# Four tags of accumulators shared out anew, row numbers read at once, and token columns written later, in one fused attention, experts and MLP kernel

## The chip, the cores and the metric

The kernel runs on one core of one Trainium2 chip. The metric is the device time of one execution in microseconds (us), the median of several executions. The engines are named as in the profile: PE is TensorE's matmul and PEld its weight load, DVE is VectorE, ACT is ScalarE, POOL is GpSimd, and SP is SyncE, which here only issues transfers.

## The reference

Three layers follow one another. The output of the first is flattened to 2304 tokens of 512 values.

```
# 1. attention, 4 x 8 heads, 576 positions of 64, causal window of 128, linear bias
scores = where(mask, q @ k.T / 8 + bias, -1e9);  x = softmax(scores) @ v
# 2. eight experts, each token goes to one of them
logits = x @ w_gate                      # 512 x 8
expert_idx = argmax(logits, axis=1);     gate_w = softmax(logits)[expert_idx]
for e in range(8):
    xe = x[expert_idx == e]
    out[expert_idx == e] = gate_w * (maximum(xe @ w1[e], 0) @ w2[e])   # 512 x 1024, 1024 x 512
# 3. one MLP for all tokens
r = maximum(out @ w_in, 0);  result = (r * r) @ w_out                  # 512 x 2048, 2048 x 512
```

## The kernel before, in words

**Three stages.** Attention takes the first 160 us or so, the experts run from there to about 377 us, and the MLP from there to the end. The experts' stage is where the change lies. Products are made of f16 halves: a value is split into a high half and a low half, and a product is three matmuls (high by high, high by low, low by high).

**Rows of an expert.** While attention runs, scatters (line 478) write each token's number into a list in DRAM, one stretch of the list for each expert. They run a second time for the last tokens ("late"), to write the gate's weight beside the number. The expert stage takes a fixed number of rows of each expert's list (384, 384, 352, 352, 304, 256, 256, 224), in pieces of 128 or fewer. `prep(e)` reads the row numbers of expert e from that list (line 989, a transfer that POOL issues). `gather(e)` turns them into indices (line 995) and fetches the tokens' rows by indirect transfers, one for each piece (line 787, POOL). `columns(e)` copies an expert's stretch of the list to the place where the last stage looks up to which token a column belongs (line 730, POOL).

**One expert.** `turn` turns a gathered piece over by eight PE transposes (line 795) into a buffer that ACT copies out (line 796). `s1` makes the first product in eight blocks, fc from 0 to 7 (lines 804 to 806). ACT writes the high half with the relu (line 807), DVE the low half (line 808). `s2` makes the second product with four accumulators side by side: in each of eight blocks, three matmuls into each of them (lines 858 to 860). At its end ACT copies the four to `yT` (line 863).

**PSUM.** Four tags a, b, c and d have two buffers each. `s1` takes a and b in turn, and the transposed pieces take d. A tag's buffers go round: whoever asks for a tag gets the older buffer, and waits until its last reader is done.

**Weights.** Each expert has eight pieces of weights. SP loads a piece (line 756), ACT writes its high half (line 778), DVE its low half (line 779). The next expert's pieces are loaded and split while the present expert computes. Between them lie the steps of `wide()`, which load and decode the weights of the third stage (line 875 loads; lines 880 to 882 and 903 to 906 are on DVE, 911 and 927 on ACT). Each engine takes its instructions strictly in its own order, which a scheduler wrote before the run: an instruction that waits holds up all behind it on that engine.

**The seam to the third stage.** During experts 6 and 7 `norm` finds scales for the outputs (line 1141 multiplies them in, on DVE) and `wide1` starts the MLP's first products (line 1187). They take PSUM through `bank`, which goes round a, b and c, or a and b alone where `self.narrow` is set.

Of the kernel before, what the change touches and what calls it, by code (L numbers as in the profile page):

```python
# [22 lines left out]
N, DM, E, F, F2 = 2304, 512, 8, 1024, 2048  # L23
P = 128
# [69 lines left out]
class K:  # L94
# [754 lines left out]
    def s2(self, ws, hts, at, n, then=None):  # L849

        nc = self.nc
        ys = [self.psum(t, [P, n]) for t in "ccab"]
        for fc in range(8):
            hh, hl = hts[fc][:, 0, :n], hts[fc][:, 1, :n]
            for d, py in enumerate(ys):
                o = fc % 2 * DM + d * P
                wh, wl = (ws[fc // 2][:, a, o:o + P] for a in range(2))
                nc.tensor.matmul(py, wh, hh, start=fc == 0, stop=False)  # L858
                nc.tensor.matmul(py, wl, hh, start=False, stop=False)  # L859
                self.last_mm = nc.tensor.matmul(py, wh, hl, start=False, stop=fc == 7)  # L860
            if fc == 7:
                for d, py in enumerate(ys):
                    nc.scalar.copy(self.yT[:, d, bass.ds(at, n)], py)  # L863
            if then is not None and fc % 2 == 1:
                then(fc // 2)
# [70 lines left out]
    def wide(self, k=1):  # L936
        def store():
            while len(self.stored) > (2 if self.steps and self.steps[0][0] != self.in_step else 0):
                self.stored.pop(0)()

        for _ in range(k):
            store()
            if self.finish:
                self.finish()
                self.finish = None
            if self.steps:
                f, *a = self.steps.pop(0)
                self.finish = f(*a)
# [23 lines left out]
    def experts(self, stack):  # L972
        nc, tc, cp = self.nc, self.tc, self.cp
        mp = self.mp = stack.enter_context(tc.tile_pool(name="mp", bufs=2))
        self.dec = mp.tile([P, 1024], U32, name="dec", bufs=1)
        self.work = mp.tile([P, 7680], F32, name="work", bufs=1)
        self.open_wide(stack)
        ids, idt, idx = self.list, self.idt, self.idx
        w = self.w_first
        wide = self.wide  # L980
        xgs = {}

        def blocks(e):
            return [(c, min(P, ROWS[e] - c * P)) for c in range(EB if e == 0 else 0, -(-ROWS[e] // P))]

        def prep(e):

            c0, c1 = blocks(e)[0][0], blocks(e)[-1][0] + 1
            dma = nc.gpsimd.dma_start(idt[:, e, c0:c1], ids[:, bass.ds(self.ev[e], 1), c0:c1].rearrange("p e a o -> p (e a) o"))
            for sc in self.scatters if e == 0 else ():  # L990
                self.behind(dma, sc)

        def gather(e):
            c0, c1 = blocks(e)[0][0], blocks(e)[-1][0] + 1
            nc.gpsimd.tensor_scalar(idx[:, e, c0:c1], idt[:, e, c0:c1, 0], float(N - 1), None, op0=ALU.min)
            xgs[e] = [self.gather_x(idx[:m, e, c:c + 1]) for c, m in blocks(e)]

        def turn(xt, e, c):
            if c < len(xgs[e]):
                g = xgs[e][c]  # L1000
                self.transpose_x(g, xt[:, :, c * P:c * P + g.shape[0]], nc.scalar.copy)

        prep(0)
        prep(1)
        gather(0)
        gather(1)
        self.places()
        with tc.issue_after(self.last_gather.ins):
            for f in self.late:
                f()  # L1010
        wide(2)
        self.s2([w[2, 0, k] for k in range(4)], self.hte, 0, EB * P, lambda d: wide())
        xt = self.new_xf(P)
        self.transpose_whole(xgs[0][0], xt)
        self.offsets()
        for e in range(E):
            W = ROWS[e] - blocks(e)[0][0] * P
            more = e + 1 < E
            if more:
                nxt = self.xt(e + 1)  # L1020
            if e == 2:
                self.overflow_table()
            if e == 7:
                for _ in self.wo_tiles(KEPT, lambda: self.ring(F16, [P, 2048])):
                    pass
            hts = []
            for fc in range(8):
                ht = self.hts(e, W)[fc]
                if e == 0:
                    self.s1_whole(fc, w[1, e, fc // 2], xt, ht, W)  # L1030
                else:
                    self.s1(fc, w[1, e, fc // 2], xt[:, :, :W], ht, W)
                hts.append(ht)
                if fc % 2 == 1 and more and e > 0:
                    w[1, e + 1, fc // 2] = self.load_w(1, e + 1, fc // 2)
                if fc in STEPS[e][0]:
                    wide()
                if fc in (3, 5, 7) and more:
                    turn(nxt, e + 1, fc // 2 - 1)
                if e == 7 and fc == 2:  # L1040
                    next(nrm)

            def then(d):
                if more:
                    w[2, e + 1, d] = self.load_w(2, e + 1, d)
                if e + 2 < E:
                    if d == 0:
                        prep(e + 2)
                    if d == 2:
                        gather(e + 2)  # L1050
                if d in STEPS[e][1]:
                    wide()
                if e == 6 and d != 2:
                    next(nrm)
                if e == 7 and d == 0:
                    with tc.issue_after(self.last_mm.ins):
                        tc.mark_branch_hint_location("overflow", "LikelyTaken", [mybir.EngineType.PE])
                if d == 3 and e < 7:
                    self.columns(e)
                    if e == 6:  # L1060
                        self.columns(7)

            self.narrow = e == 6
            if e == 6:
                nrm = self.norm(0, 24576, 14336)
            if e == 7:
                self.wide1(0, 0)
            self.s2([w[2, e, k] for k in range(4)], hts, self.off[e], W, then)
            xt = nxt

# [309 lines left out]
    def moe2(self):  # L1380
        NG, tc = NT // GT, self.tc
        self.overflow()
        nrm = {1: self.norm(1, 7168, None)}
        next(nrm[1])

        def first(k):
            self.wide()
            next(nrm[1])

        self.load_columns()  # L1390
        self.wide1(0, 1, first)
        self.turn_columns()
        while self.finish:
            self.wide()
        self.fetch_out()
        def at(*key):
            for n in MIXES.get(key, ()):
                if n in mixing:
                    for _ in mixing.pop(n):
                        pass  # L1400
                else:
                    mixing[n] = self.mix(n)
                    next(mixing[n])

        mixing = {}
        for G in range(NG):
            more, far = G + 1 < NG, G + 2 < NG
            nr = nrm[G + 2] = self.norm(G + 2, None, None) if far else iter([None] * 9)

            def step():  # L1410
                with tc.issue_after(self.end_act.ins), tc.issue_after(self.end_dve.ins):
                    next(nr)

            if G < SG:
                self.wide2(G, 0, lambda k: step() if k != 1 else None)
            else:
                self.seven(G, 0, lambda k: step() if k == 5 else None)
            at(G, 0)
            if more:
                self.wide1(G + 1, 0, lambda k: step() if k == 0 or G >= SG and k == 1 else at(G, 1) if k == 1 else None)  # L1420
            if G < SG:
                self.wide2(G, 1)
                if G + 1 == SG:
                    self.narrow = True
            else:
                self.seven(G, 1, lambda k: step() if k in (0, 1) else None)
            at(G, 2)
            if more:
                self.wide1(G + 1, 1, lambda k: step() if G >= SG and k == 0 else None)
            at(G, 3)  # L1430
# [60 lines left out]
```

## Time and profile before

| | |
|---|---|
| time, median of 3 runs | 748.61 us (748.33 to 751.21) |
| time of the profiled execution | 751.45 us |
| its span, first to last instruction | 749.6 us |
| mean granted TensorE clock | 0.984 of full speed |
| PE busy | 712.6 us, 95% |
| DVE busy | 576.8 us, 77% |
| ACT busy | 468.8 us, 63% |
| POOL busy | 206.5 us, 28% |

The span is what the trace holds; 1.85 us of the execution lie outside it. A row of a timeline says when an instruction started, how long it took, its engine, its line, what it wrote and read, and in brackets how long the engine had been idle before it and what ended the wait. A busy share over the whole span is a mean over three stages with different limits, so the rows below are from the stretch from 169 us to 377 us.

### The profile page before, as it was taken

What the parts mean: (1) busy time and instruction counts of PE and PEld (TensorE: products, weight loads), DVE (VectorE), ACT (ScalarE), POOL (GpSimd) and SP (SyncE); (2) the same over time, 40 slices, a digit from 0 to 9 for tenths busy, and PEclk for the clock granted to TensorE, in tenths of its full rate; (3) what the DMA queues carried; (4) which work ended last, traced back from release to release, by engine and by line L of the source; (5) the groups of instructions that cost most, each with busy time, mean ns of one, the idle gap of its engine ahead of it and who ended that gap; (6) DMA issues with size and microseconds to landing.
All of it is one profiled execution on the core that took longest, in us unless ns stands there. A gap on an engine that the chain in (4) does not pass through costs nothing. (4 is left out here: it accounts for less than half of the span.)

```text
span 749.6 us, 19619 instructions
## 1 busy us (share of the span) xinstructions
PE 712.6 (95%) x7979; PEld 603.5 (81%) x7979; DVE 576.8 (77%) x1442; ACT 468.8 (63%) x772; POOL 206.5 (28%) x247
## 2 busy tenths in 40 slices
PE   6899999999888999999999999999999999999996
PEld 5799899888655666788898566677899999999995
DVE  5788888864778999969986966758678787878672
ACT  5688888943457655657555664656657575757561
POOL 4573522345252401000000245523411111111011
PEclk9899999989999999999999999999999999999998
DMA  8798203876899887367704000000000000000000
GB/s 299 289 365 234 81 29 68 278 163 172 239 305 299 283 263 240 125 220 241 241 5 141 31 26 6 2 30 1 30 2 30 2 30 2 30 2 30 2 30 29
DMA packets 37416, 91.71 MB, mean 122 GB/s; under 512 B 5305, under 2 KB 16075, under 8 KB 37307
## 3 DMA queue, kind: packets, MB, share of 16 engines
q1 hardware_dynamic: 31563, 75.77, 32.1%
q0 software_dynamic: 5760, 14.65, 6.0%
q8 instruction: 64, 1.05, 0.6%
q14 instruction: 29, 0.24, 0.1%
HBM read 77.54 MB, written 13.04 MB: 121 GB/s over the span
## 5 line engine op out<-in xcount | busy, mean ns | idle before, releaser
L1187 PEld LDWEIGHTS <-wi 128*128 128x128 f16 x3024 | 170.6, 98 | 3.6 <-issue 2.3
L1323 PEld LDWEIGHTS <-wr 128*128 128x128 f16 x1008 | 98.1, 98 | 12.1 <-issue 0.7
L1187 PE MATMUL ps_a<-work,wi 128*128 128x128 f16 x1344 | 84.2, 219 | 0.0
L1187 PE MATMUL ps_b<-work,wi 128*128 128x128 f16 x1272 | 79.7, 219 | 0.4 <-ACTq L1075 0.4
L1211 DVE TENSOR_TENSOR wr<-work,wr 128x1024 f16<-128x1024 f32 (+1 forms) x72 | 70.4, 1001 | 11.0 <-ACT wr L1210 10.8
L1215 ACT ACTIVATE work<-work 128x1024 f32<-128x1024 f32 x36 | 38.1, 1057 | 54.8 <-DVE work L1207 54.8
L315 PE MATMUL ps_a<-yT,wr 128*128 128x192 f32 (+2 forms) x288 | 66.6, 352 | 5.4 <-DMA wr<-in_q_dram 5.2
L1210 ACT CAST wr<-work 128x1024 f16<-128x1024 f32 (+1 forms) x72 | 59.9, 832 | 17.1 <-DVE work L1230 7.6
L327 ACT ACTIVATE pb<-pb,nm 128x192 f32<-128x192 f32 (+2 forms) x144 | 56.5, 433 | 11.6 <-DVE nm L320 10.8
L320 DVE CUSTOM_DVE_ANT_0 pb<-ps_a,bias 128x192 f32<-128x192 f32 (+2 forms) x144 | 44.4, 327 | 16.1 <-PE ps_a L315 10.2
L778 ACT ACTIVATE wr<-rw 128x1024 f16<-128x1024 f32 x40 | 42.2, 1058 | 22.1 <-DMA rw<-in_w_dram 21.5
L1351 POOL DMA_INDIRECT out_dram<-o,oid x18 | 25.8, 1436 | 102.0 <-ACT o L1349 67.4
L779 DVE SCALAR_TENSOR_TENSOR wr<-rw,wr 128x1024 f16<-128x1024 f32 x40 | 48.8, 1221 | 5.0 <-ACT wr L778 5.0
L315 PEld LDWEIGHTS ps_a<-yT,wr 128*128 128x128 f32 x288 | 47.1, 206 | 6.4 <-DMA yT<-in_k_dram 5.5
L1286 POOL TENSOR_TENSOR yT<-wr 128x512 f32<-128x512 f16 x8 | 10.4, 1294 | 148.9 <-ACTq L1075 116.0
L338 PE MATMUL ps_b<-cst,pb 128*128 128x128 f32 x256 | 45.1, 288 | 0.5 <-ACT pts L342 0.4
L804 PE MATMUL ps_a<-work,wr 128*128 128x352 f16 (+4 forms) x112 | 34.1, 304 | 7.0 <-ACT yT L863 5.6
L1216 ACT ACTIVATE work<-work 128x1024 f32<-128x1024 f32 x36 | 38.0, 1057 | 1.1
L787 POOL DMA_INDIRECT xg<-xd,idx x21 | 26.8, 1274 | 35.6 <-PE ps_d L795 26.5
L1235 DVE TENSOR_TENSOR work<-work 128x512 f32<-128x512 f32 x18 | 13.3, 739 | 29.8 <-ACT work L1204 29.8
L859 PEld LDWEIGHTS <-wr 128*128 128x128 f16 x288 | 28.2, 98 | 9.8 <-issue 2.6
L858 PE MATMUL ps_c<-work,wr 128*128 128x352 f16 (+5 forms) x128 | 35.9, 283 | 0.0
(307 smaller groups left out, 2005.8 us busy)
## 6 DMA issues: line engine op xcount, KB each, us to landing
rw<-in_w_dram SPq DMA_DIRECT2D x40, 512.0 KB, 5.4
wi<-in_w_dram SPq DMA_DIRECT2D x20, 512.0 KB, 5.0
rw<-in_wo_dram SPq DMA_DIRECT2D x16, 512.0 KB, 4.7
rw<-in_wi_dram SPq DMA_DIRECT2D x32, 256.0 KB, 5.2
wr<-in_q_dram SPq DMA_DIRECT2D x14, 512.0 KB, 12.8
xd<-xhl POOLq DMA_DIRECT2D x16, 256.0 KB, 7.8
rw<-in_v_dram SPq DMA_DIRECT2D x12, 325.0 KB, 6.4
yT<-in_k_dram SPq DMA_DIRECT2D x4, 576.0 KB, 8.7
```

The source lines that it names most:

```text
L315: nc.tensor.matmul(ps[:, s, first:hi], q[g, u, hh // 4][:, hh % 4, s if u < 4 else 0, :], self.kt[g, hh // 2][:, hh % 2, key0:key0 + hi - ...
L320: self.last_ttr = nc.vector.tensor_tensor_reduce(out=pb[:, s, first:hi], in0=ps[:, s, first:hi], in1=self.bias[:, hh, first - lo:192], sca ...
L327: self.last_exp = nc.scalar.activation(pb[:, s, first:hi], pb[:, s, first:hi], AF.Exp, bias=nm[:, s:s + 1], scale=-1.0)
L338: nc.tensor.transpose(pt[:, t, :, s, :], pb[:, s, t * P:(t + 1) * P], self.idf)
L778: self.nc.scalar.activation(t[:, 0], st, AF.Copy, scale=sc)
L779: self.nc.vector.scalar_tensor_tensor(t[:, 1], st, sc, t[:, 0], op0=ALU.mult, op1=ALU.subtract)
L1187: self.nc.tensor.matmul(ps[:, j], w[:, kp, a, w0 * P:(w0 + 1) * P], v[:, 2 * x + kp], start=kp + b == 0, stop=kp == 1 and b == 2)
L1210: self.end_act = self.fin_act = nc.scalar.copy(hi, src)
L1211: self.end_dve = self.fin_dve = V.tensor_tensor(lo, src, hi, op=ALU.subtract)
L1215: nc.scalar.activation(ci, ci, AF.Relu)
L1216: nc.scalar.activation(ci, ci, AF.Square, scale=0.5)
L1323: nc.tensor.matmul(ps[n], x[:, v, j], y[j][:, w], start=m + i + j == 0, stop=m == 1 and i == 2 and j == 3)
```

## The change

The second product's accumulators are taken from tags c and d (two each) and no longer from c, a and b. The transposes of the next expert's pieces, also in d, come after blocks 2, 4 and 6 instead of 3, 5 and 7 (for expert 0 they stay). The row numbers of all eight experts are read one after another before the first gather, and no longer two experts ahead. The token columns are written at the end of experts 5 and 6. `bank` takes only a and b during both experts 6 and 7.

```diff
     def s2(self, ws, hts, at, n, then=None):
...
-        ys = [self.psum(t, [P, n]) for t in "ccab"]
+        ys = [self.psum(t, [P, n]) for t in "ccdd"]
...
         prep(0)
-        prep(1)
+        for e in range(1, E):
+            prep(e)
         gather(0)
         gather(1)
...
-                if fc in (3, 5, 7) and more:
-                    turn(nxt, e + 1, fc // 2 - 1)
+                if more and fc in ((3, 5, 7) if e == 0 else (2, 4, 6)):
+                    turn(nxt, e + 1, (fc + 1) // 2 - (2 if e == 0 else 1))
...
                 if e + 2 < E:
-                    if d == 0:
-                        prep(e + 2)
                     if d == 2:
                         gather(e + 2)
...
-                if d == 3 and e < 7:
-                    self.columns(e)
-                    if e == 6:
-                        self.columns(7)
-
-            self.narrow = e == 6
+                if d == 3:
+                    for f in {5: range(6), 6: (6, 7)}.get(e, ()):
+                        self.columns(f)
+
+            self.narrow = e >= 6
...
         self.overflow()
         nrm = {1: self.norm(1, 7168, None)}
+        self.narrow = False
```

Where an instruction stands is decided by the scheduler, so the diff alone does not show it. Lines above 1041 keep their numbers; those from 1126 to 1375 are two lower in the changed kernel, so that line 1141 becomes 1139.

The first place is POOL's order as the experts' stage begins: the reads of row numbers (L989), the conversion to indices (L995), the gathers (L787, into buffers `xg`). Before, the last of the two reads and what follows it:

```order
L989 ISA
L989 DMA ids_385<-ids_77 128x3x2
L995 TENSOR_SCALAR idx_386<-ids_385 128x1
L787 DMA xg_3356<-xd_76,idx_386 128x1024
L995 TENSOR_SCALAR idx_386<-ids_385 128x3
L787 DMA xg_3359<-xd_76,idx_386 128x1024
L787 DMA xg_3361<-xd_76,idx_386 128x1024
```

And now, the last of the eight reads and what follows it:

```order
L989 ISA
L989 DMA ids_385<-ids_77 128x2x2
L995 TENSOR_SCALAR idx_386<-ids_385 128x1
L995 TENSOR_SCALAR idx_386<-ids_385 128x3 x3
L787 DMA xg_3362<-xd_76,idx_386 128x1024
L787 DMA xg_3365<-xd_76,idx_386 128x1024
L787 DMA xg_3367<-xd_76,idx_386 128x1024
L787 DMA xg_3369<-xd_76,idx_386 128x1024
```

Six reads were put ahead of the first gather, and so were the conversions for experts 1, 2 and 3, which wait for the reads to land. The copies of the columns still stand soon after the first gathers in POOL's order.

The second place is ACT's order in the first product of expert 1: splits of weights (L778, from `rw` or a borrowed `wi` buffer), the relu (L807), the copies of the transposed pieces (L796, 96 columns for the last piece of expert 2). Before:

```order
L778 ACTIVATE wr<-rw 128x1024 x2
L807 ACTIVATE work<-ps_a 128x384
L778 ACTIVATE wr<-rw 128x1024
L927 ACTIVATE wi_3352<-dec 128x512
L807 ACTIVATE work<-ps_b 128x384
L796 COPY work<-ps_d 128x8x128
L778 ACTIVATE wr<-wi_3349 128x1024
L807 ACTIVATE work<-ps_a 128x384
L807 ACTIVATE work<-ps_b 128x384
L778 ACTIVATE wr<-rw 128x1024
L796 COPY work<-ps_d 128x8x96
```

Now:

```order
L807 ACTIVATE work<-ps_a 128x384
L778 ACTIVATE wr<-rw 128x1024
L796 COPY work<-ps_d 128x8x128
L778 ACTIVATE wr<-rw 128x1024
L807 ACTIVATE work<-ps_b 128x384
L927 ACTIVATE wi_3352<-dec 128x512
L778 ACTIVATE wr<-wi_3349 128x1024
L807 ACTIVATE work<-ps_a 128x384
L796 COPY work<-ps_d 128x8x96
L807 ACTIVATE work<-ps_b 128x384
L778 ACTIVATE wr<-rw 128x1024
```

The last piece's copy moved ahead of the last relu of the expert and of one split, and stands right behind the relu of block 6.

The third place is the same stretch one expert later, in the first product of expert 2. Before:

```order
L778 ACTIVATE wr<-rw 128x1024
L807 ACTIVATE work<-ps_a 128x352
L911 ACTIVATE wi_3346<-dec 128x896
L807 ACTIVATE work<-ps_b 128x352
L778 ACTIVATE wr<-wi_3352 128x1024
L796 COPY work<-ps_d 128x8x96
```

Now:

```order
L778 ACTIVATE wr<-rw 128x1024
L807 ACTIVATE work<-ps_a 128x352
L796 COPY work<-ps_d 128x8x96
L911 ACTIVATE wi_3346<-dec 128x896
L807 ACTIVATE work<-ps_b 128x352
L778 ACTIVATE wr<-wi_3352 128x1024
```

The copy moved ahead of a decode step, a relu and a split, but still stands behind one split (L778) that reads a loaded piece. SP's order of loads is the same in both kernels, and DVE's differs by single places.

## Rows read from the trace of the kernel before

**Rows 1.** The page: its span, and the busy time of PE.

```profile
span 749.6 us, 19619 instructions
...
PE 712.6 (95%) x7979; PEld 603.5 (81%) x7979; DVE 576.8 (77%) x1442; ACT 468.8 (63%) x772; POOL 206.5 (28%) x247
```

**Rows 2.** The waits of PE, 180 to 380 us: total, times, longest.

```profile
PE ps_a L804 <- ACT yT L863: 5.6, 4, 2.1
PE ps_d L795 <- DMA xg<-xd,idx: 3.8, 2, 3.4
```

**Rows 3.** PE's timeline at the end of each of its long waits.

```profile
206.21 0.72 PE L795 MATMUL ps_d<-id,xg 128*128 128x128 f16 x8 [3.37 <-DMA xg<-xd,idx]
...
220.38 0.32 PE L858 MATMUL ps_b<-work,wr 128*128 128x384 f16 x1 [1.82 <-DVE work L808]
...
240.37 0.31 PE L804 MATMUL ps_a<-work,wr 128*128 128x352 f16 x1 [2.11 <-ACT yT L863]
...
254.02 0.32 PE L858 MATMUL ps_c<-work,wr 128*128 128x352 f16 x1
...
273.50 0.31 PE L804 MATMUL ps_a<-work,wr 128*128 128x352 f16 x1 [1.41 <-ACT yT L863]
...
373.78 0.26 PE L804 MATMUL ps_a<-work,wr 128*128 128x224 f16 x1 [1.66 <-ACT yT L863]
...
376.74 0.26 PE L804 MATMUL ps_a<-work,wr 128*128 128x224 f16 x1 [0.50 <-DVE yT L1141]
```

**Rows 4.** Windows: busy time (instructions) of each engine, granted clock, DMA share.

```profile
206.00:210.00 4.00, 3.79 (x19) 2.10 (x20) 3.25 (x6) 2.42 (x4) 2.77 (x3) 0.57 0.86 251
210.00:214.00 4.00, 4.00 (x32) 2.58 (x31) 2.19 (x3) 1.82 (x3) 2.14 (x2) 1.00 0.97 341
240.50:244.00 3.50, 3.50 (x14) 1.86 (x13) 3.50 (x12) 3.40 (x5) 1.35 (x2) 0.53 0.56 147
260.00:270.00 10.00, 10.00 (x70) 6.56 (x68) 9.83 (x17) 4.31 (x6) 0.00 (x0) 1.00 0.84 263
```

**Rows 5.** POOL's timeline: the first reads and gather, then expert 2's read.

```profile
169.60 1.42 POOL L989 DMA_DIRECT2D ids<-ids  x2 [4.65 <-DMA ids<-tok,pos]
...
175.76 1.07 POOL L787 DMA_INDIRECT xg<-xd,idx  x1 [0.56 <-POOL idx L995]
...
195.30 0.82 POOL L989 DMA_DIRECT2D ids<-ids  x1 [8.01 <-DMA ids<-tok,pos]
```

**Rows 6.** Line 989 alone: nanoseconds of one on POOL, and until it landed.

```profile
L989 POOL DMA_DIRECT2D ids<-ids x8: 568/780/835, 169.6 to 227.4; - x8
...
DMA to landing us min/median/max: 4.3/5.4/6.9
```

**Rows 7.** ACT's timeline in the first products of experts 1 and 2.

```profile
217.20 1.07 ACT L778 ACTIVATE wr<-wi 128x1024 f16<-128x1024 f32 x1
218.16 0.49 ACT L807 ACTIVATE work<-ps_a 128x384 f16<-128x384 f32 x1
...
255.47 1.06 ACT L778 ACTIVATE wr<-rw 128x1024 f16<-128x1024 f32 x1 [4.16 <-DMA rw<-in_w_dram]
256.44 0.44 ACT L807 ACTIVATE work<-ps_a 128x352 f16<-128x352 f32 x1
...
258.91 0.79 ACT L796 COPY work<-ps_d 128x768 f16<-128x768 f16 x1
```

**Rows 8.** SP's timeline: the load that the split at 255.47 us waits for.

```profile
251.30 0.34 SPq L756 DMA_DIRECT2D rw<-in_w_dram  x1
```

**Rows 9.** Transfers issued from 221.2 to 222.3 us: KB, us to landing.

```profile
wi<-in_w_dram SPq DMA_DIRECT2D x1, 512.0 KB, 7.0
```

**Rows 10.** DVE's timeline at the seam to the third stage.

```profile
373.68 0.43 DVE L880 TENSOR_SCALAR dec<-rw 128x512 uint32<-128x512 uint32 x1
...
375.47 1.21 DVE L1141 TENSOR_TENSOR yT<-yT,ps_a 128x1024 f32<-128x1024 f32 x1
```

**Rows 11.** DVE's low half for block 0 of expert 2.

```profile
243.73 0.51 DVE L808 SCALAR_TENSOR_TENSOR work<-ps_a,work 128x352 f16<-128x352 f32 x1
```

## The prediction

> **What bounds the kernel now.** I read the page first. PE is busy for 712.6 of 749.6 us [rows 1], so only PE's stalls can be won back, and whatever is not on PE's path costs nothing. Next I read PE's waits in the stretch that the change touches. Two kinds matter: blocks of the first product that wait for ACT's copies to `yT` (5.6 us, four times), and transposes that wait for gathers (3.8 us, twice) [rows 2]. PE's timeline places them [rows 3]: 3.37 us at 206.21 (a gather of expert 2), 1.82 us at 220.38 (fourth accumulator of expert 1), 2.11 us at 240.37 and 1.41 us at 273.50 (first block of experts 2 and 3), 1.66 us at 373.78 (expert 7). The change aims at these.
>
> The windows then say what such a wait costs beyond itself [rows 4]. Behind the 3.37 us wait the granted clock is 0.57, and 19 matmuls run in 4 us where the next 4 us hold 32: 13 lost at 4/32 us is 1.6 us. Behind the 2.11 us wait the clock is 0.53, with 14 matmuls in 3.5 us where 70 in 10 us would make 24.5: 10.5 at 0.143 us is 1.5 us. These windows are also why the stalls aren't simply there to be taken. DVE is busy for 9.83 of 10 us and the DMA share is 0.84 to 0.97 in three of the four windows. ACT and DVE split the next expert's weights there in a fixed order, behind loads. ACT stands 4.16 us for one load at 255.47 [rows 7], issued at 251.30 [rows 8], which is 4.17 us earlier.
>
> **Row numbers read at once.** Before, the first gather issues at 175.76, behind two reads that begin at 169.60 [rows 5]. Now six more reads stand ahead, and also the conversions for experts 1 to 3. A read takes POOL 0.78 us and lands 5.4 us (4.3 to 6.9) later [rows 6]. The fourth read begins at 169.60 + 3 x 0.78 = 171.9 and lands at 177.3. With the 0.56 us that a gather waits for its conversion [rows 5] the first gather issues at 177.9: **+2.1 us** (+1.0 to +3.6 by the landing's extremes), all of it on PE, which waits for its first piece.
>
> The skill bears on this step. POOL's rows have 0.57 to 0.84 us for each read [rows 6]. The Trainium skill, "DMA: Bandwidth & Descriptors", section "Anatomy of one DMA — SWDGE (gpsimd) path", says that many descriptors can be emitted before their incremental cost shows, the fixed part being mostly completion. By that the six reads would come free and this term would be nothing. The rows speak against it, since POOL is held for each.
>
> In exchange expert 2's gather no longer stands behind a read that waits 8.01 us, to 195.30, for the late scatters [rows 5]. Its last piece then arrives before PE needs it: the 3.37 us wait and its 1.6 us at half clock go, **-5.0 us**. PE reaches the second product of expert 1 by 2.1 - 5.0, 2.9 us sooner.
>
> **Accumulators in d, pieces one block sooner.** Tag d has two buffers. Three pieces take them in turn, so the third accumulator waits for the copy of the second piece, and the fourth for the copy of the third. Before, only the next piece of an expert waited for such a copy; now PE itself does in the middle of its work.
>
> Expert 1: the third copy (0.79 us [rows 7]) stands behind a split at 217.20 and a relu that ends at 218.65, so it ends about 219.4, and the fourth accumulator starts 1.0 us sooner than at 220.38. That split shows no wait, and in the new order another piece's copy no longer stands right ahead of it, so all this may come up to 0.8 us sooner. But PE came 2.9 us sooner, and now stands 1.82 + 2.9 - 1.0 = 3.7 us, no less than in the wait that ended at half clock [rows 3, 4]: 1.6 us back. **Between -1.8 and +0.6 us in all, where -2.9 was brought in.**
>
> Expert 2, first block: the 2.11 us wait and its 1.5 us go, since tags a and b are no longer held by accumulators. But block 4 reuses block 0's buffer, which DVE frees at 243.73 + 0.51 [rows 11] in a queue without gaps. I give the block **-1 us**; by the next step it doesn't matter.
>
> Expert 2, second product: this is the step on which the sum rests. Before, PE started at 254.02 [rows 3], and the fourth accumulator nine matmuls later, at 254.02 + 9 x 0.143 = 255.3. Now it waits for the third copy. ACT's order puts that right behind the split that waits for its load until 255.47, and the relu behind it: 256.44 + 0.44 + 0.79 = 257.7, less the 0.1 us by which neighbours on ACT overlap in these rows (255.47 + 1.06 against 256.44): 257.6. PE's position is set by that, whatever it gained before: **+2.3 us** against before. If DVE runs a microsecond sooner, the load's buffer is freed and the load issued that much sooner: +1.3. If the stall ends at half clock as at 240.37: +3.8. The nearest row by length, 2.11 us, has the half clock, but 1.82 us and 1.66 us have no such stretch behind them, so I take none.
>
> The skill has a rule for that. The Trainium skill, "TensorE: Matmul & The Clock Gate", section "HAM oscillation — how this bites in real kernels", says that waits for data between groups of matmuls let the clock fall back to half, and that each next group then starts cold. By it the sum below would be 1.5 us higher. Two rows agree (0.57 and 0.53 [rows 4]), and no row decides for a wait of this size.
>
> Expert 3, first block: the 1.41 us wait for `yT` goes, **-1.4 us**; 0.9 us of the shift stays. From expert 3 on ACT's copies come in time, as ACT is busy for 4.31 of 10 us [rows 4], and PE carries the shift along.
>
> Expert 7: the 1.66 us wait goes, but block 2 still waits for DVE's multiply (ends at 375.47 + 1.21 = 376.68, and PE goes on at 376.74 [rows 3, 10]). So the gain is nothing, and since that multiply stands one L880 later in the changed order, **+0.4 us** (0.43 [rows 10]; nothing if DVE has a gap there). `wide1` on two tags asks for a buffer again only four products later; I cost it at nothing, its cover being the matmuls between. Without that cover one drain by DVE (1.21 us at most [rows 10]) would be seen once. The columns' copies leave POOL's way late in the stage and nobody on PE waits for them: nothing.
>
> **Sum.** +2.3 - 1.4 + 0.4 = +1.3 us; what lies ahead of expert 2's second product is swallowed by its wait. The profiled execution took 751.45 us, 2.84 above the median of 748.61, and its span is 749.6. The shift is a difference of times in one trace, so I put it on the median: **749.9 us**. With the lower value of the step, +0.3 (748.9); with the higher, +2.8 (751.4). About 0.5% (3.7 us) is what a measurement of this kernel can tell from no change: 744.9 to 752.3.
>
> **Rivals.** (1) The copies keep up: a sooner PE pulls DVE, the load and the split along, so that the fourth accumulator isn't late. Then -1.4 + 0.4, and up to 1 us of what came before: 746.6 to 747.6. For it: the splits behind a sooner relu. Against it: the split waits for a load, not for PE.
> (2) The whole loop of loads, splits and buffers runs sooner, and most stalls are won. All of them: 3.37 + 1.6 + 1.82 + 2.11 + 1.5 + 1.41 + 1.66 = 13.5, less 2.1 and 0.4, is -11.0: 737.6. Half of that gives 743.1. For it: PE's order frees a and b at every seam, and one gather's wait was the first stall of the chain. Against it: DVE at 9.83 of 10 us [rows 4].
> (3) Slower: the load that the split at 255.47 waits for lands later, because the loads of a sooner PE and more gathers crowd together. One of the same size took 7.0 us [rows 9], not 4.17. The stall grows by 2.8 to 5.1 us and surely ends at half clock, 1.5 more: +1.3 + 2.8 + 1.5 = +5.6, 754.2. It decides from a landing of about 5.1 us, where 1.3 + 1.5 + 0.94 passes 3.7. For it: the crowded windows. Against it: SP's order is unchanged.
> (4) The change doesn't do what it says: the columns "late" stand early in POOL's order anyway. That would alter nothing.
>
> **How the numbers follow.** Forecast 0.44 (its own range 748.9 to 751.4), rival 1 0.14, rival 2 0.26, rival 3 0.16. Faster by over 0.5% is rival 2: 0.26. Slower is rival 3: 0.16. The rest, 0.58, is within. The range reaches into both: from 742.0, which leaves out the deeper half of rival 2 (0.13), to 754.2, which leaves out the upper part of rival 3 (0.06).
>
> **What the profile after would show.** The first gather near 178 and no wait for `xg` of expert 2 at PE: the reads were costed rightly. A row of PE in `ps_d` (L858) with a wait for ACT's L796 at the second product of experts 1 and 2, about 3.7 and 2.3 us: the step that the sum rests on. No such rows, or rows under 1 us, make rival 1 or 2 right; then PE's waits for `yT` are gone and DVE or a load ends what is left. A wait of 5 us there with a clock near 0.5 behind it is rival 3. I would be wrong if the copies were ready sooner than ACT's fixed order lets me see, or if a stall opened where none is now.

## The result: 1.4% slower

The changed kernel takes 759.15 us (758.71 to 761.77, 4 runs), the kernel before 749.91 us beside it (748.33 to 751.58, 4 runs). The ratio is 1.0141, 95% interval 1.0117 to 1.0165: about 10 us slower (9.2 us by the medians, 10.6 by the ratio), outside the range that was forecast. The page of the changed kernel:

```profile
span 759.8 us, 19623 instructions
...
PE 717.3 (94%) x7979; PEld 605.0 (80%) x7979; DVE 578.6 (76%) x1442; ACT 468.1 (62%) x772; POOL 202.2 (27%) x247
```

PE is busy for 4.7 us more with as many instructions [rows 1], and the span is 10.2 us longer. Against a second trace of the kernel before (run e9 below, PE busy for 710.3 of 751.4 us) it is 7.0 of 8.4 us. So part of the loss is waits and part is the same matmuls taking longer, but the two traces don't agree on the shares. PE's waits from 160 to 400 us have new names:

```profile
PE ps_d L858 <- ACT work L796: 8.1, 4, 4.0
PE ps_a L804 <- DVE yT L1139: 3.1, 1, 3.1
PE ps_a L804 <- DVE work L808: 2.6, 5, 0.9
PE ps_d L795 <- ACT yT L863: 1.9, 1, 1.9
```

Every wait of [rows 2] above 1 us is gone, as the change meant. In their place PE waits in the second product for the copy of a transposed piece, once with a transpose for the copies to `yT`, and at the seam to the third stage for DVE. PE's timeline places the long waits, with two landmarks between them, the starts of the second product of expert 3 (290.30) and of the first product of expert 7 (381.04):

```profile
220.84 0.48 PE L858 MATMUL ps_d<-work,wr 128*128 128x384 f16 x1 [3.97 <-ACT work L796]
...
259.19 0.45 PE L858 MATMUL ps_d<-work,wr 128*128 128x352 f16 x1 [3.70 <-ACT work L796]
...
290.30 0.31 PE L858 MATMUL ps_c<-work,wr 128*128 128x352 f16 x1
...
361.85 0.61 PE L795 MATMUL ps_d<-id,xg 128*128 128x128 f16 x8 [1.90 <-ACT yT L863]
...
381.04 0.26 PE L804 MATMUL ps_a<-work,wr 128*128 128x224 f16 x1
...
386.58 0.26 PE L804 MATMUL ps_a<-work,wr 128*128 128x224 f16 x1 [3.08 <-DVE yT L1139]
```

In the trace of before the first landmark is this row, the second stands in [rows 3] (373.78):

```profile
285.52 0.32 PE L858 MATMUL ps_c<-work,wr 128*128 128x352 f16 x1
```

The same two in the second trace of the kernel before (e9):

```profile
287.66 0.32 PE L858 MATMUL ps_c<-work,wr 128*128 128x352 f16 x1
...
375.33 0.26 PE L804 MATMUL ps_a<-work,wr 128*128 128x224 f16 x1 [1.79 <-ACT yT L863]
```

The landmarks split the 10.2 us (8.4 against the second trace) into three. Up to expert 3's second product the changed kernel loses 4.8 us (2.6). From there to expert 7 it takes 90.7 us where before took 88.3 (87.7): 2.5 us (3.1). The rest takes 378.8 where before took 375.8 (376.1): 2.9 us (2.7). The two traces of before differ by 2.1 us in the first part alone, so that part can't be read more closely than that.

**The clock behind the long waits.** Windows of 4 us of the changed kernel behind the two longest and behind the one at 386.58 (busy time and instructions of PE, PEld, DVE, ACT and POOL, granted clock, DMA share, GB/s):

```profile
221.00:225.00 4.00, 4.00 (x14) 1.81 (x13) 4.00 (x9) 1.23 (x2) 0.49 (x1) 0.50 0.90 233
225.00:229.00 4.00, 4.00 (x21) 2.16 (x20) 0.85 (x3) 0.87 (x1) 0.03 (x1) 0.78 0.96 350
...
259.50:263.50 4.00, 4.00 (x15) 2.07 (x14) 3.77 (x6) 1.79 (x3) 0.00 (x0) 0.50 0.73 272
263.50:267.50 4.00, 4.00 (x25) 2.51 (x24) 3.96 (x7) 1.06 (x1) 0.00 (x0) 0.90 0.75 247
...
386.50:390.50 4.00, 3.92 (x25) 3.30 (x25) 3.95 (x11) 2.47 (x5) 0.00 (x0) 0.59 0.00 0
```

The same places in the kernel before, at full clock:

```profile
220.50:224.50 4.00, 4.00 (x26) 2.40 (x25) 3.90 (x9) 1.48 (x2) 3.38 (x4) 1.00 0.93 292
259.00:263.00 4.00, 4.00 (x29) 2.61 (x28) 4.00 (x6) 2.72 (x4) 0.00 (x0) 1.00 0.75 240
...
376.70:380.70 4.00, 3.96 (x42) 3.96 (x42) 4.00 (x11) 2.43 (x6) 0.00 (x0) 1.00 0.02 5
```

Expert 1: 12 + 5 matmuls fewer than 26 in each 4 us, at 4/26 us, is 2.6 us. Expert 2: 14 + 4 fewer than 29, at 4/29 us, is 2.5 us. The granted clock is 0.50, the lower of its two levels, 1.2 GHz. So the two waits cost 3.97 + 2.6 and 3.70 + 2.5, 12.8 us in all; they took the place of stalls of before that cost nearly as much (3.37 + 1.6 + 1.82 + 2.11 + 1.5 + 1.41 = 11.8 us by [rows 3, 4]). Expert 7: 17 matmuls fewer than 42, at 4/42 us, is 1.6 us, behind the wait of 3.08 us.

**What lies ahead of the second wait.** ACT's rows there, and the load that its split waits for on SP:

```profile
257.05 1.06 ACT L778 ACTIVATE wr<-rw 128x1024 f16<-128x1024 f32 x1 [4.01 <-DMA rw<-in_w_dram]
258.01 0.45 ACT L807 ACTIVATE work<-ps_a 128x352 f16<-128x352 f32 x1
258.35 0.79 ACT L796 COPY work<-ps_d 128x768 f16<-128x768 f16 x1
```

```profile
252.95 0.34 SPq L756 DMA_DIRECT2D rw<-in_w_dram  x1
```

This is the row that the sum rested on: split, relu, copy, and PE goes on at 259.19. The load took 4.10 us to land, as before (4.17), but was issued 1.65 us later than in [rows 8]. In both traces it is issued 0.12 us after a low half of DVE (L779) ends, at 252.83 here and at 251.18 before. PE had begun this expert's first product at 237.9 in place of 234.5, behind the wait in expert 1; that the one delay follows from the other is read from these times, not shown by a run.

**What lies ahead of the later losses.** ACT's rows at the ends of experts 3, 5 and 6: the copies to `yT` (L863) and the steps of `wide()` between them (L911, L927). The last row of each end shows the last copies:

```profile
303.53 0.45 ACT L863 COPY yT<-ps_c 128x352 f32 x1 [1.02 <-PE ps_c L860]
306.89 0.95 ACT L911 ACTIVATE wi<-dec 128x896 f16<-128x896 f32 x1 [2.91 <-DVE dec L906]
...
308.08 0.81 ACT L863 COPY yT<-ps_d 128x352 f32 x2
...
357.73 0.63 ACT L863 COPY yT<-ps_c 128x256 f32 x2
360.59 0.95 ACT L911 ACTIVATE wi<-dec 128x896 f16<-128x896 f32 x1 [2.23 <-DVE dec L906]
361.44 0.63 ACT L863 COPY yT<-ps_d 128x256 f32 x2
...
380.82 0.35 ACT L863 COPY yT<-ps_c 128x256 f32 x1
383.59 0.63 ACT L927 ACTIVATE wr<-dec 128x512 f16<-128x512 f32 x1 [2.42 <-DVE dec L882]
...
384.37 0.65 ACT L863 COPY yT<-ps_d 128x256 f32 x2
```

A step that waits 2.2 to 2.9 us for DVE's decode stands among four copies that have nothing to do with it. The first copy is done (in expert 5 the first two); the others come 3 to 4 us later, behind the step. Before, expert 3 had such a step among its copies too, behind the first two; experts 5 and 6 had none:

```profile
301.73 0.95 ACT L911 ACTIVATE wi<-dec 128x896 f16<-128x896 f32 x1 [2.06 <-DVE dec L906]
```

PE pays for this only in part where it waits for the copies themselves (1.90 us at 361.85). From the first landmark to the second it also waits 3.5 us for low halves (L808), where the two traces of before have 0.8 us of such waits in the first product.

### The profile page after: what moved, and what is told of

It reads as the page before. It is cut to its first block, busy times and chain, and to the rows that moved or that the text cites. A ratio compares the mean times of both kernels' runs of the same rounds, so it can differ in the third digit from the quotient of the medians.

```text
span 759.8 us, 19623 instructions
## 1 busy us (share of the span) xinstructions
PE 717.3 (94%) x7979; PEld 605.0 (80%) x7979; DVE 578.6 (76%) x1442; ACT 468.1 (62%) x772; POOL 202.2 (27%) x247
## 5 line engine op out<-in xcount | busy, mean ns | idle before, releaser
L1185 PE MATMUL ps_b<-work,wi 128*128 128x128 f16 x1320 | 82.7, 219 | 0.3 <-PEq L1073 0.3
L778 ACT ACTIVATE wr<-rw 128x1024 f16<-128x1024 f32 x40 | 42.3, 1060 | 20.5 <-DMA rw<-in_w_dram 16.3
L779 DVE SCALAR_TENSOR_TENSOR wr<-rw,wr 128x1024 f16<-128x1024 f32 x40 | 48.8, 1220 | 3.3 <-ACT wr L778 1.9
L858 PE MATMUL ps_d<-work,wr 128*128 128x352 f16 (+5 forms) x128 | 37.0, 292 | 8.1 <-ACT work L796 8.1
L859 PEld LDWEIGHTS <-wr 128*128 128x128 f16 x288 | 28.7, 100 | 17.4 <-issue 10.1
L858 PE MATMUL ps_c<-work,wr 128*128 128x352 f16 (+5 forms) x128 | 37.1, 293 | 0.0
L860 PE MATMUL ps_d<-work,wr 128*128 128x352 f16 (+5 forms) x128 | 37.1, 292 | 0.0
```

The lines of the kernel that those rows point to most:

```text
L779: self.nc.vector.scalar_tensor_tensor(t[:, 1], st, sc, t[:, 0], op0=ALU.mult, op1=ALU.subtract)
L1185: self.nc.tensor.matmul(ps[:, j], w[:, kp, a, w0 * P:(w0 + 1) * P], v[:, 2 * x + kp], start=kp + b == 0, stop=kp == 1 and b == 2)
```

## The experiments

Theory A is that of the prediction, made larger: the accumulators in d wait for ACT's copies, and the half clock follows. Theory B puts the loss on POOL's order, theory C on ACT's copies of pieces that now stand ahead of relus. In each comparison "slower" is against the kernel before of the same set of runs; 0.1% is 0.75 us. "Better than the changed kernel" is the difference of two such ratios from two sets, and is uncertain by 2 to 3 us.

**Parts of the change alone** (e1 to e4). The first kernel has `"ccdd"`, the pieces one block sooner and `narrow`; the second the reads at once and the columns late; the third only the first and last of these lines, the fourth only the middle one:

```diff
-        ys = [self.psum(t, [P, n]) for t in "ccab"]
+        ys = [self.psum(t, [P, n]) for t in "ccdd"]
...
-                if fc in (3, 5, 7) and more:
-                    turn(nxt, e + 1, fc // 2 - 1)
+                if more and fc in ((3, 5, 7) if e == 0 else (2, 4, 6)):
+                    turn(nxt, e + 1, (fc + 1) // 2 - (2 if e == 0 else 1))
...
-            self.narrow = e == 6
+            self.narrow = e >= 6
```

> Before, with the accumulators in c and d, the transposes one block sooner and the narrow bank, but with the row numbers and the token columns as before. Theory A (the fourth accumulator, in d, waits for ACT's copy of the next expert's third piece, and PE then runs at half clock): this part alone carries the loss, 8 to 11 us slower than before, with PE waits for L796 of about 8 us in all. Theory B (the reads, gathers and columns on POOL come at worse times): within 2 us of before. Theory C (copies put ahead of relus in ACT's order make the low halves late): 8 to 11 us slower as well, but told apart by the two next runs.

Measured: 1.0124 (1.0107 to 1.0140), 10 us slower. PE waits 4.5 us for L796 and 5.7 us for L808. The loss is in this part. Theory B falls: what the rest of the change adds is 1.3 us, uncertain by 2.2.

> Before, with all row numbers read at once and the token columns written late, and nothing else. Theory A: the wait of 3.4 us for expert 2's gather goes and the first gather is 1 to 2 us later; between 5 us faster and 1 us slower. Theory B: 8 us or more slower. Theory C: as theory A.

Measured: 1.0033 (1.0014 to 1.0052), 2.5 us slower, a little outside theory A's bounds. The wait for expert 2's gather is gone, but PE then waits 3.67 and 1.84 us for DVE's low halves in the next product, and before that 2.42 and 0.73 us for the first pieces. Behind both the clock is low (0.50 from 221 to 225 us, 0.59 from 181.3 to 185.3). What this part wins is swallowed there.

> Before, with the accumulators in c and d and the narrow bank, the transposes left after blocks 3, 5 and 7. Theory A: the third piece is turned over only after the last block, so its copy comes later still than in the changed kernel and the fourth accumulator waits for 4 to 6 us in experts 1 and 2: 10 to 16 us slower than before. Theory B: within 2 us. Theory C: less than 3 us slower.

Measured: 1.0046 (1.0029 to 1.0063), 3.4 us slower, where theory A asked for 10 to 16. PE's largest wait in that trace:

```profile
PE ps_d L858 <- ACT work L796: 7.4, 4, 4.1
```

The waits of theory A are there, nearly as long as in the changed kernel, and the kernel loses less than half of what they last. That stalls of before are gone in exchange is the likely reason. From expert 3's second product to the end this trace takes 463.6 us (285.48 to 749.1), as long as before (464.1 and 463.7), so `narrow`, which has no run of its own, shows no cost there.

> Before, with the transposes one block sooner and nothing else; the accumulators stay in c, a and b. Theory A: nothing in PE's path waits for the copies, within 2.5 us of before. Theory B: the same. Theory C: 5 to 10 us slower, with PE waits for DVE's low halves (L808) of 5 us or more.

Measured: 1.0085 (1.0068 to 1.0102), 6.4 us slower. The time is the one that theory C names, but the wait isn't:

```profile
PE ps_a L804 <- ACT yT L863: 11.9, 5, 3.1
...
PE ps_b L858 <- DVE work L808: 0.7, 1, 0.7
```

PE hardly waits for low halves and waits 11.9 us for the copies to `yT`, where before it was 5.6 [rows 2]. So the part that only theory C had at fault carries the larger share, and by another way: its trace has decode steps among these copies, as shown above for the changed kernel. At the ends of experts 3, 5 and 6 the steps wait 4.04, 2.29 and 2.41 us for DVE, and PE then waits 2.50, 2.53 and 3.06 us for the copies; the first of them:

```profile
300.50 0.95 ACT L911 ACTIVATE wi<-dec 128x896 f16<-128x896 f32 x1 [4.04 <-DVE dec L906]
...
302.19 0.29 PE L804 MATMUL ps_a<-work,wr 128*128 128x304 f16 x1 [2.50 <-ACT yT L863]
```

That became theory D.

**The decode steps behind the copies** (e5 to e7). In the fourth kernel, in before and in the changed kernel, a step's ACT instruction is issued only behind the last copy to `yT`:

```diff
             if self.finish:
-                self.finish()
+                with self.tc.issue_after(self.last_y.ins) if self.last_y is not None else nullcontext():
+                    self.finish()
...
-                    nc.scalar.copy(self.yT[:, d, bass.ds(at, n)], py)
+                    self.last_y = nc.scalar.copy(self.yT[:, d, bass.ds(at, n)], py)
```

> The transposes one block sooner alone, as in the run before, and each decode step's ACT instruction issued only behind the four copies to yT. Theory D (what the sooner transposes cost is a decode step that now stands between the copies to yT at the ends of experts 3 and 6, 4 us each in the trace): the 6.9 us go, so from 3.5 us faster to 0.5 us slower than before, with PE waits for L863 under 4 us in place of 11.9. Theory C (copies of pieces ahead of relus make the low halves late): still 5 to 7 us slower.

Measured: 1.0044 (1.0018 to 1.0070), 3.3 us slower. The wait for L863 fell to 1.5 us, the time by 3.1 us (uncertain by 2.3), half of what was expected. Part of the rest may be gathers, for which PE waits 6.7 us in this trace and 3.8 in [rows 2].

> The kernel before, with only the decode steps' ACT instructions issued behind the four copies to yT. Theory D: PE's waits for L863 (5.6 us) mostly go, 1 to 5 us faster than before. Rival: DVE and the loads pace this stretch, so the stall only moves to PE's waits for L808: within 1 us of before.

Measured: 1.0037 (1.0015 to 1.0058), 2.8 us slower. Theory D's gain isn't there. The edit costs something of its own: in expert 7 PE waits 2.2 us (`ps_c` of `wide1`) and 1.3 us for DVE's work on the inputs and sums of the third stage, which it didn't before, and in expert 6's first product it still waits 2.8 us for the copies. Seen against this kernel (752.49 us, same set) the last one (752.52) loses nothing that shows: with the copies together the sooner transposes cost nothing, within some 2.5 us.

> The changed kernel with the decode steps' ACT instructions issued behind the four copies to yT. Theories A and D together: 3 to 6 us faster than the changed kernel, so 4 to 7 us slower than before; the wait of 3.1 us for the yT multiply in expert 7 goes, the waits of 4 us for L796 in experts 1 and 2 stay. Theory A alone: within 1 us of the changed kernel.

Measured: 1.0060 (1.0026 to 1.0094), 4.5 us slower than before and 6 us better than the changed kernel. The wait for the `yT` multiply in expert 7 is gone, as theory D has it; in its place PE waits 1.3 us for scales. The waits of theory A stay and are longer in total, as PE's waits show (L859 and L797 are L858 and L796 here, one line lower):

```profile
PE ps_d L859 <- ACT work L797: 9.4, 4, 3.7
```

ACT at the end of expert 3 (L864 is the copy, L912 the step):

```profile
300.65 0.90 ACT L864 COPY yT<-ps_c 128x352 f32 x2 [1.19 <-PE ps_c L861]
301.55 0.90 ACT L864 COPY yT<-ps_d 128x352 f32 x2
302.35 0.95 ACT L912 ACTIVATE wi<-dec 128x896 f16<-128x896 f32 x1
```

The copies follow one another in 1.8 us where they took 5.4. Of the change's loss of 1.4% some 0.8 goes with them.

**Theory A taken away** (e8). The pieces come earlier still, and the split stands behind the piece's copy:

```diff
+                if more and e > 0 and fc in (1, 3, 5):
+                    turn(nxt, e + 1, fc // 2)
                 if fc % 2 == 1 and more and e > 0:
-                    w[1, e + 1, fc // 2] = self.load_w(1, e + 1, fc // 2)
+                    with self.tc.issue_after(self.last_turn.ins):
+                        w[1, e + 1, fc // 2] = self.load_w(1, e + 1, fc // 2)
```

> The changed kernel with the pieces turned over after blocks 1, 3 and 5, and the split of the next weights in the same block issued on ACT behind the piece's copy. Theory A: the third copy no longer stands behind a split that waits for its load, so PE's waits for L796 fall from 8.1 us to under 1.5, and the time is 4 to 7 us better than the changed kernel, 3 to 6 us slower than before. Rival: the split and with it the weights come later by as much, PE waits elsewhere, within 1.5 us of the changed kernel.

Measured: 1.0133 (1.0096 to 1.0171), no better than the changed kernel. PE's waits:

```profile
PE ps_d L795 <- ACT yT L863: 7.4, 4, 4.0
PE ps_a L1141 <- DVE sd L1136: 5.3, 1, 5.3
...
PE ps_d L858 <- ACT work L796: 2.5, 2, 2.2
```

The wait for L796 fell to 2.5 us, and PE reached the second product of expert 3 at 285.29, 5.0 us sooner than the changed kernel. That much bears theory A out. It was lost again at later seams: an earlier piece waits for the buffer that the copy to `yT` still holds, and the scales of the third stage came late.

**The kernel before again** (e9), nothing edited.

> The kernel before, unchanged, for a second trace and for what two sets of runs of one kernel differ by. Both theories: within 0.4% of before; its trace places the 2 to 3 us by which the first trace of before lies above the median (expected between 180 and 300 us, where loads set the pace).

Measured: 1.0004 (0.9976 to 1.0033). One kernel against itself lies within 0.3%; its trace is the second one quoted above.

**Both edits** (e10): those of e7 and e8 together.

> The changed kernel with both edits: pieces turned over after blocks 1, 3 and 5 with the split behind the piece's copy, and the decode steps behind the copies to yT. Theories A and D (two causes that add up): no 4 us wait for L796 at expert 2, no loss at the ends of experts 3 and 6, so 9 to 12 us better than the changed kernel, between 2 us faster and 2 us slower than before. Rival (each stall that is taken away comes back at the next seam, since loads, ACT and DVE pace the stretch): 2 to 6 us better than the changed kernel at most.

Measured: 1.0061 (1.0044 to 1.0079), no better than the copies together alone. But the two edits together didn't take theory A's waits away: PE still waits 4.3 us for L797 (the copy of a piece, one line lower), and 2.7 us for a copy to `yT` and 3.9 us for the scales. So this run doesn't show whether the two causes add up.

**The pair in d lags** (e11, e12). In `s2` the accumulators in c run four blocks ahead, and their copies to `yT` come as much sooner (the lines that move the copies and the next loads are left out here):

```diff
+        order = [(k, (0, 1)) for k in range(4)]
+        for k in range(8 - 4):
+            order += [(k, (2, 3)), (k + 4, (0, 1))]
+        order += [(k, (2, 3)) for k in range(8 - 4, 8)]
+        for i, (fc, ds) in enumerate(order):
+            block(fc, ds)
```

> The changed kernel with the second product's pair in d lagging four blocks behind the pair in c, so that 24 matmuls (3.4 us) lie ahead of the first use of d. Theory A: the wait for L796 of 4.0 and 3.7 us in experts 1 and 2 falls under 1 us and the half clock behind it goes: 4 to 7 us better than the changed kernel, the loss from expert 3 on stays. Rival: PE waits the same time elsewhere, within 1.5 us of the changed kernel.

Measured: 1.0082 (1.0054 to 1.0110), 4.4 us better than the changed kernel, as theory A has it. The two waits and the window behind the first:

```profile
220.54 0.32 PE L859 MATMUL ps_d<-work,wr 128*128 128x384 f16 x1 [0.78 <-ACT work L796]
...
258.91 0.31 PE L859 MATMUL ps_d<-work,wr 128*128 128x352 f16 x1 [1.04 <-ACT work L796]
```

```profile
220.60:224.60 4.00, 4.00 (x26) 2.38 (x26) 3.41 (x7) 1.33 (x2) 0.56 (x2) 1.00 0.94 255
```

Short waits, the second a little above what was asked, and the clock stays at 1.00, its upper level of 2.4 GHz. PE reaches expert 3's second product at 285.57, as before (285.52 and 287.66). From there to the end it takes 468.1 us, so the later loss stays, as said. One new wait came, 2.84 us at 240.12 for the copies to `yT`, with a clock of 0.58 behind it.

> The lagging pair with the decode steps behind the copies to yT. Theories A and D: 9 to 13 us better than the changed kernel, between 3 us faster and 2 us slower than before. Rival: 3 to 6 us better than the changed kernel, no better than with the copies together alone.

Measured: 1.0034 (1.0012 to 1.0056), 8 us better than the changed kernel, short of the 9 that theories A and D asked for but within the uncertainty, and 2.5 us slower than before. Here too theory A's wait came back (L797 is the copy of a piece), with a clock of 0.57 behind the longest:

```profile
PE ps_d L860 <- ACT work L797: 6.4, 3, 3.9
```

No variant beat the kernel before.

**Theory D by itself** (e13, e14) **and theory A without it** (e15). In the kernel before, a step is put behind the first copy and ahead of the other three at the ends of experts 3, 5 and 6; in the changed kernel the steps go behind the copies at those three ends alone; in the third kernel the accumulators and `narrow` stand alone with all copies together. The first of these edits:

```diff
                 for d, py in enumerate(ys):
-                    nc.scalar.copy(self.yT[:, d, bass.ds(at, n)], py)
+                    if d == 1 and self.cur in (3, 5, 6) and self.finish:
+                        with self.tc.issue_after(y.ins):
+                            self.finish()
+                        self.finish = None
+                        self.hold = self.last_dec
+                    with self.tc.issue_after(self.hold.ins) if d and self.hold is not None else nullcontext():
+                        y = nc.scalar.copy(self.yT[:, d, bass.ds(at, n)], py)
```

> The kernel before, where at the ends of experts 3, 5 and 6 a decode step's ACT instruction is put behind the first copy to yT and ahead of the other three, as it came to stand in the changed kernel. Theory D (it is the decode step between the copies that costs, whatever else is changed): 4 to 8 us slower than before, with PE waits for L863 of 2 us or more at the starts of experts 4, 6 and 7. Rival (the copies stand apart because the loop of loads and splits is already late there, and their place costs nothing by itself): within 2 us of before.

Measured: 1.0027 (1.0003 to 1.0050), 2.0 us slower (0.2 to 3.8), where theory D asked for 4 to 8. Theory D as worded falls: the place alone costs less than that, and the longest wait for the copies at the three ends is 1.0 us. ACT's rows suggest why (L870 is the copy, L919 the step):

```profile
297.68 0.95 ACT L919 ACTIVATE wi<-dec 128x896 f16<-128x896 f32 x1
298.53 0.45 ACT L870 COPY yT<-ps_c 128x352 f32 x1
```

Here the step didn't wait, nor at the two other ends. Its decode was ready, and it held the copies for its own 0.9 us, where in the changed kernel it held them for 2.91 us more.

> The changed kernel with the decode steps behind the copies to yT only at the ends of experts 3, 5 and 6. Theory D: as with all ends, 4 to 8 us better than the changed kernel. Rival (the gain of that run came from experts 1 and 2, whose loads then came sooner): within 2 us of the changed kernel.

Measured: 1.0079 (1.0054 to 1.0103), 4.7 us better than the changed kernel (uncertain by 2.6), from three ends alone. The wait for the `yT` multiply in expert 7 is gone here too. The landmarks show where the gain lies:

```profile
292.94 0.31 PE L859 MATMUL ps_c<-work,wr 128*128 128x352 f16 x1
...
380.57 0.26 PE L805 MATMUL ps_a<-work,wr 128*128 128x224 f16 x1
```

From the first landmark to the end (756.2) this is 463.3 us, and 463.7 in e7. The changed kernel takes 469.5, before 464.1 and 463.7. With the steps behind the copies the whole of the later loss is gone; what is left of the change's loss lies ahead of expert 3's second product.

> The accumulators in c and d and the narrow bank alone, with the decode steps behind the copies to yT. Theory A (waits for L796 cost what they last): 0.3 to 0.6% slower than before with the copies together, so 0.6 to 1.0% slower than before. Rival (PE catches these waits up before expert 4, since loads set the pace of experts 1 to 3): 0.2 to 0.5% slower than before, as with the copies together and nothing else.

Measured: 1.0095 (1.0063 to 1.0128), 7 us slower. The accumulators in d cost time without the decode steps among the copies too: 0.6% over before with the copies together, 0.5% in e3.

## Why the prediction was wrong

Its mechanism came about and was sized too small, and a second one wasn't seen. Point by point:

**The reads at once.** The first gather was put at 177.9 and issued at 177.42, and PE waited for the first pieces (1.15 and 0.88 us). Right, but for the clock behind these waits: it was 0.58 from 182.5 to 186.5 us, with 26 matmuls where before has 38, which is 1.3 us. The wait for expert 2's gather is gone. Right.

**Expert 1.** A wait of 3.7 us was given, 3.97 measured, with the half clock at 2.6 us instead of 1.6. The length of the wait is partly luck: PE reached the second product at 215.13, 1.8 us sooner than before and not 2.9, and the third copy (at 219.99, 0.79 us long) ended at 220.8 and not at 219.4.

**Expert 2, the step on which the sum rested.** PE waits for the copy behind the split behind the load, as said. But the wait was put at 2.3 us without half clock, and measured 3.70 us and 2.5 us. The load was taken to be issued at 251.30 as before; in the changed order it was issued at 252.95. This term was mis-sized by about 4 us. The rival by the late load had the right consequence by the wrong cause: the landing took 4.10 us, not 7.0.

**Expert 3, first block, -1.4 us.** Right: PE has no such wait there, and the first product takes 15.6 us (274.68 to 290.30) in place of 17.2. Up to here the sum closes with the measured sizes: 2.3 + 1.4 + 2.5 - 1.4 = 4.8 us, which is what the first landmark shows (2.6 against the second trace of before).

**The Trainium skill's clock rule.** By the Trainium skill, "TensorE: Matmul & The Clock Gate", section "HAM oscillation — how this bites in real kernels", a wait for data between groups of matmuls is followed by a cold stretch. The windows agree with the rule at the waits of 3.97 and 3.70 us (clock 0.50) and of 3.08 us (0.59), while those of 0.78 and 1.04 us in e11 show full clock. The prediction had priced such a stretch at 1.5 us and left it out of its sum.

**"From expert 3 on ACT's copies come in time ... and PE carries the shift along."** This step failed. The copies of pieces do come in time; the copies to `yT` don't. The order that I had read for two places on ACT was different in a third, the ends of experts 3, 5 and 6, and there a decode step that waits for DVE holds three copies or two, and all that stands behind them on ACT. From expert 3's second product to the end the changed kernel takes 469.5 us where before took 464.1 and 463.7: 5.4 to 5.8 us that the sum had at 0.4, and that go when the steps stand behind the copies (e7, e14). Of these, 2.5 to 3.1 us lie ahead of expert 7.

**Expert 7, +0.4 us.** The row measured was 3.08 us in place of 0.50, and 1.6 us of half clock behind it; the 1.66 us wait of before is gone. The rest of the trace is 2.7 to 2.9 us longer. DVE's rows ahead of the multiply (L1139):

```profile
384.25 0.69 DVE L928 SCALAR_TENSOR_TENSOR wr<-dec,wr 128x512 f16<-128x512 f32 x1 [0.69 <-ACT wr L927]
384.98 0.43 DVE L880 TENSOR_SCALAR dec<-rw 128x512 uint32<-128x512 uint32 x1
385.32 1.21 DVE L1139 TENSOR_TENSOR yT<-yT,ps_a 128x1024 f32<-128x1024 f32 x1
```

The multiply follows DVE's own part of the decode without a gap; the last copies to `yT` end at 385.02. So it stands behind the step that ACT and DVE share (L927 and L928), by DVE's order as much as by the copies; no run parts the two. One L880 more was the prediction's reading; that the multiply also comes behind the step's low half (L928), which waits for ACT, wasn't seen. That `wide1` on two tags costs nothing agrees with e3's trace.

So shown by runs: the part in PSUM carries the loss (e1), and its two halves both cost (e3, e4). Moving the decode steps out from among the copies takes 4.7 to 6 us off the changed kernel (e7, e14), and the traces place this gain from expert 3 on. Letting the pair in d lag takes 4.4 us off (e11), ahead of expert 3's second product; that the wait for L796 costs this much agrees with e3 and e15, whose edits hold more than the wait. Argued only: that it is the step's wait and not its place that costs. For it stand e13, where steps that don't wait cost 2.0 us, and e4, where steps that wait cost more. That such a wait isn't charged in full is seen in the kernel before itself: at the end of expert 3 a step waits 2.06 us among the copies, and PE doesn't wait for them (in e4 it waits 2.50 us there, behind a step that waited 4.04). Open: whether the two causes add up, since neither e10 nor e12 took theory A's waits away. Nor is it settled why the same edit costs 2.8 us in the kernel before (e6), and why e2 alone is 2.5 us slower.

## What to carry to other kernels

When an edit lets a scheduler write a new order, read the whole order of the engine that empties PSUM, not only at the places the edit names: an unrelated instruction that waits, set among the copies that free a buffer, can be charged to whoever needs the buffer or what comes behind the copies. A freed wait in a stretch paced by loads came back here at a later seam (e2, e8), so price the seam behind it before the stall that goes. A wait in the middle of PE's work is to be counted with the half-clock stretch behind it, once rows of the same length show one: here every wait of PE of 3 us or more in the experts' stage of before (two traces) and of the changed kernel had one, at a granted clock of 0.50 to 0.59.

## What the runs showed that was not expected

The half clock lasted longer here than in [rows 4]: 17 and 18 matmuls were lost behind waits of 3.97 and 3.70 us, where 13 were lost behind 3.37 us. For shorter waits the length alone doesn't tell. Waits of 1.04 us and less in e11 left the clock at 1.00, but the changed kernel's 1.15 and 0.88 us for the first pieces were followed by 0.58; in e4 the clock was 1.00 behind a wait of 2.46 us and 0.57 behind one of 2.50. One kernel measured twice in a set agreed within 0.3%, but two traces of it lay 2.1 us apart at one landmark, in the stretch where loads set the pace; that is as much as several of the differences asked for above.
